# A complex linear recurrence and an MLP on one core: the two turned copies of a channel in neighbouring partitions, one load for the phases, and another order of all steps

## The chip, the core and the metric

The kernel runs on one core of one Trainium2 chip. The core has five instruction queues that run beside each other, each in its own order: TensorE (PE in the profile; its weight loads are PEld), VectorE (DVE), ScalarE (ACT), GpSimd (POOL) and SyncE (SP), which here issues every transfer. Sixteen DMA engines move the data. The metric is the device time of one launch in microseconds. Before the change it was 854.92 us in the median of three runs (851.49, 854.92 and 858.98).

## What is computed

First a gated linear recurrence for 4 batches, 8 heads, 768 tokens and 48 channels, with a complex gate per token and channel whose magnitude is held under 0.999; then a two-layer MLP on the result, with a leaky activation:

```
mag = np.sqrt(a_re * a_re + a_im * a_im)
scale = np.minimum(mag, 0.999) / (mag + 1e-06)
a_re_n, a_im_n = (a_re * scale, a_im * scale)
for t in range(S):                       # S_re, S_im: 48x48 for each batch and head
    new_re = ar * S_re - ai * S_im
    new_im = ar * S_im + ai * S_re
    S_re, S_im = (new_re + k[t] v[t]^T, new_im)
    y[t] = q[t] . S_re
x = y as (3072 tokens, 384)
h = x @ w_in                             # 384 -> 2048
out = (max(h, 0) + alpha * min(h, 0)) @ w_out
```

## The kernel before

**The recurrence.** Each batch is cut into 6 chunks of 128 tokens, so there are 24 units, (batch, chunk). In a unit the product of gates over a stretch of tokens is split in a magnitude (the decays) and a turn (the phases). A real 96-row problem replaces the complex 48-row one: q and k lie in a tile twice, 48 channels in partitions 0 to 47 and the same 48 again in partitions 48 to 95. The first copy is multiplied by the real part of the phase, the second by the imaginary part (L665, L667), and the matmuls sum over all 96 partitions. The six levels `LEVELS` (1, 2, 4, 8, 16, 32) multiply by decays on VectorE (L721), meet keys and queries on TensorE (L682, into `ps_lv`), mask (L703 on ScalarE, L706 on VectorE), and apply the values (L821, into `ps_y`). Keys are transposed (L789, copied by ScalarE at L791 and L792), and the state `St` goes on from chunk to chunk (L801, L830, L833, L845). The 48 rows of y are copied out (L859) and written to a DRAM scratch `ysc` (L864).

**The gates.** `gates` makes decays and phases for a whole batch or half of one, with 128 channels in partitions: 9 calls, A to I in the order, of 1, 2, 3 and then six times 3 chunks. It writes them to DRAM scratch tiles: `decs` (L324) and `phs` (L432, with the first token's value at L422). For batch 0 its small operations run on VectorE, for the others on GpSimd: products of 8 by 8 tokens (L339, L341), then a short serial recurrence over the tile `run`, six steps of an L339 and an L341 on 12 and 6 elements per partition for a call of 3 chunks. ScalarE hands it its input (`runs<-gate`, L367 and L369) and takes its output (`runs<-run`, the same lines a little later).

**The loads.** `loads` brings a unit's operands: q and k from the inputs into `KQ` (L580, L582; two copies each of 192 KB), phases from `phs` into `PP` (L591, two loads of 193.5 KB, real part into partitions 0 to 47, imaginary into 48 to 95), and decays from `decs` into `T` (L598, the same 384 KB twice). `KQ` has 3 buffers, `T` 2, `PP` 1. `loads_v` brings values in token order and spread by level (`V`, `VL`), `half_rows` makes a DRAM scratch `vsc` for some of these. `pieces` and `weights` load the float64 weights as words (L492) and turn them into float32 (L508, L510, L512 on ScalarE, L516 on GpSimd, L518, L520 on VectorE).

**The MLP.** `loads_x` loads a group of 128 or 256 tokens (L877). `all_mlp` runs over 14 groups: for each of 16 features blocks, three matmuls (L893, `ps_h`, two buffers), the activation by ScalarE (L900) and VectorE (L902) into `g_sb`, then the second layer's matmuls (L912, `ps_o`), and the result goes out (L922, L925).

**The order.** Each of these functions is a generator that yields before each step. `ORDER` is a string of 4316 letters; a letter names a generator (A to I gates, J loads, K half_rows, L loads_v, M pieces, N and O the weights, P to Z and a to m the 24 units, n loads_x, o the MLP) and lets it go one step on. So the string fixes the order of all instructions on all five queues. The arguments of the yields (costs, rings) are not used when the string is run.

Of the kernel before, what the change touches and what calls it, by code (L numbers as in the profile page):

```python
# [27 lines left out]


ORDER = (  # L30
    "AAAAAAAAAAAAAAAAAAAAABAAAAJMJJMABBBMMBANJMMAOAAAAAAAAAAAAAAAAAALLLNBLAAAAAAAAAAALNAAAAAAAKKKKKKKLLLA"
    "OALLAMNNAAAAAAOAAAAAAAAABLBNAAAAAAALAANBBNOOBNBBBLBMBBBJJOJNOBBBBBNBBJNNNBBNBBBBOBBBBBBBBBBBBBBBNOPB"
    "POBPPPPCCCBOKBBBBBBBBBBBBBPPOBBPKBCBBBMPCBPKKBCBJKKOPOPBBBBBBOMBKPNPMBBKNJBCKBBBBPPMBKKNKKBBNBPBBBBP"
    "PBCCBPPOPCCCPPPNNPPCCCCPPCPPPPJLPPPPPJNCJPCNNNCCJNCNCCQJQJPQJDDJJCPCJMNCNCPCPCPPCOCQQPDQDDJPPPPOCOOO"
    "CJKQCQCCCCCCQQCCCCCMOQCOJCJRCCRCOQOCOQQCQCOOOCCCCCCNNKKMMCCOCQCRCQCQCNNNKCLLLLLLQLCCCCCRQOCnCDCCCOCO"
    "CCCCQRMLLNDCJQCNRNRLLCQCCLLLRMCQCQDQRJJOCOCKQODCCCCRDNQQQQCCQQQQQQJODMQLNNDQODDODoQEKoooooooDOoRooND"
    "JoooooooDRRQQRQLLoooDNoooJLoRLLLLLDRLOQNQooQoQLooRRoRoDDoQDQDOOLDoooDDoRDELDLRRRRORRRRRJDooDDDDDDDRo"
    "ooRNNooDDRooooooEoRDRRRRRDNDoDoESDSDRDJOSREKOoooooLnoLLKoRSoooRRRRSSOLLKLSSSooESRLooooooLRoSOLLoLJEL"
    "LSooNJSSSSoEoEESSDooDDooDDDDDDooooDDDDDDDKJREEoooDDDDooEDDDSDDoEooEoooSSSRSSSoLSooooJJSJETSJSJJooKJS"
    "oEoooDDDDDDooDESDSoooSSSDDDSSJEEoEETSSSSDESSSoSSSTEoooooooJJJoKoEooDSDTooooEoSoTUKTLoTTTLoooooooooLT"  # L40
    "LoLoDKUooooooLDDTDJJooooJJnKDDDoEEooooDooTTETooDooooooLUoooooooooEoTToooUUDDLoooooooDTooToooooooDLDU"
    "UUooooooUTUUooooooUoTTTTEoUUTTTTEooTTUToLLLLoooEEEToLooTTTTTTJJTTUoUUoTTUJoEooTETTTTTJKEUUUUUFooooEU"
    "oooLLVooEoUooLLLELULLUVUoTUTVooUEEoooEULLLLLoooUUUJJJFEEUUUUUJJVVVUVVooooVVVJoUUUUUVVooFVooooUooVVoV"
    "FFVVoFVLLVooEEEEEEEEEEEEEEEEoooEEEEoooooFFJJoWVLLVWJFVoooJooooVooVVVVVWVoLVFooWoFoEEEoEVoVLWWLLLLLLE"
    "LLVWVnVooJJEEEEEEJJFWooFEEEEEoWWoFFVFVJVFWVJVoFoVooooooEWEWFVLVLVWWVWVVVVoooLKLooLLLoLLLJFFWWoXoWLJo"
    "EEoEEELEoooooEooJooWWoEWEWWWEoooWEoEoooWWooFoWoWFoooooEXWWoooooLXoFoooooFFXoLXXWWWWXXWXFEXWXWWWXJJoo"
    "oooJXXJJXFWXXFFFFoWWWWWoXoXooLoooWooooooXWLXXXXXooFoooXXFYoLLFFFFFFFoXXooXoXXoooLLLLLLLoooLLLYXXXJJX"
    "FJXFFFFFFFFFFFooXYGooXXXGooYoooXXnFYJXXYYoFooYYXXXXYGooooYJJJooooooooooJoJJYFFFFooJoooJooYYYYLGGoGZY"
    "YoooooooGGoFFFFFFFooooFoYZoooFooFFoZooooZYYZYYZGYYZZoYYYoGZoYFFoYoooKKLLoYLLLLZLoLLLJLFFFFFLFLFFoZGG"
    "YoooooGZooGGoGGYYoYYJJJYoKKYGooYFFoFKKYoYLYLYLFLLLLYYLLLLFGaGZoYZFYYYFZZLZGKooooZooooLLoZKooFFFFFooo"  # L50
    "ooZZZZaZZZZZooooZZoooooZooZoooJJFFGnooJoZZZZZFFFLooLFFZLZoZJLLLoGoaaGooooooooaZZaaGGJoGoooaooaLHaHao"
    "oGGoooGGGooaooooooooZZaZGGZZZoZaaaaaGGoooaHJoGoooooooaaaoaGGaaGaaaoooooGGaoLoaLoJJoooooHHGboGGGGGGGa"
    "oHoaooLLobooLLoooooJHHabJabHaaaaaabaJbJJaJaJaHaaabbbbbbbbHJKoooooooHoooooooJGGGGoGGbbbHbGGooocGGGGbJ"
    "HoooooooooooJGGGKoooHbbccoooooooooobbccbGGGHcGbobbbGcGoooGGGGGGGGGHccooobbHGbGKLooooHHboobLLJLLLLLoL"
    "LLLLbLKnoobbcccHbbHJbcbcGHHHbHHbbcJoHHLLLLLLooLoLJLLHHHcooooocccHHoooooooooHGGGGbbbbbbbboGccccccGGoc"
    "GJGooocLoooooGocLoccooooocLLGoGHGGooocJoooocGcccccccccccccJcccooKdooHooHoooJJJoHHHoJooHHHodHHHHooooo"
    "ooooooHHHHdHHHHHooHHdoodddJdJJddddJJooeooooooooooooddoodddoooeoooddHHoooooooooHddeeeeoHHHHHLHHHHHHHL"
    "LLdddLLLLLdLLLLoJLooeeddddodooHHddoJJeoooHdddHdddddneoooHHoIddeeeeeoodeJJfLfIHdHHdHeddddooooeHooooLL"
    "LLooooooJJoooIIoooeooooIoooHoHHHooeeIoeeeHHHLfILoooHIooLooeIofHeJJoeooeooooIfffefoooeeLofoLoLoeLLLee"
    "eeeeeeoJHfKHJJooooooofeoILLfooIeeHffffKLLLfoeJLooeeeeeooooooofoooooooofoooLoofKffgooooffffffIffLILLL"  # L60
    "LJooIgHooooLfLfoooIooIKKIIIIoffffIfJnJfJHgfgJofIJJoooooooJfoooooogIfggfgoLoooffIIfLfffIogoKoggoooooo"
    "ooooooohhoogoooogggggoIhJhggoooooLoJoooooooooohhLJJooooghggggggghohogIILIIoogIoooggIogLLLLooooooIohh"
    "hhhooooLLLLgIoKKgggggggggJJJhhooohogggLIoooooooooIIIIIIKKoooogoghoJIoooooioooLooooiJJIIoooooonIIIooh"
    "hhoiioooIIIIIoIhhhIIhhhLLLLLLLhhhiJiooILLLLLooIhJooohiohhooIIooooiiJhhhhhhIhIIiohooooiooLoLiLLLILiJI"
    "hhIhhhhhJiiIiiiiooIIIIIIIIIoooooooooooLiiiiIoIooooohhiiiiiioooJjiooIIIIoooooIIoLjJJjjLooooLIooLiLoLL"
    "IjjjooooIooijjjjIIoooooooiiiIiIIiiooiLooioooLLLiLLILoLLLIIjoiiijjoiiiioooIiojoooooooooojjjoooooooono"
    "jjjoooojjLjjjjjoooooIjLjLLooooooojjoojjjjjjoooJJJJJJoooJJoojJJjoooookokkJJoooooooooooojkjkLLjjjkjjoj"
    "jkkoJkkJoJJJkoookooooLLLooooooooJlJlkkooooooooookokklooklokooooooloolkkkkokkklllLooookookLkoloLJkooo"
    "ooooooLLkLLkLoLoooollkkkkkkkkkkkkkkkoooooooooollllllooJoooooookkolooooollollJmmnJJloooooooomooollooo"
    "oooooollmllooooommllooooooooooLLoLLoLoooLLLLLoLLLLooooomooooooommmmmoooollllllooolloooooolllllllllmm"  # L70
    "oooooooooLooLLLoooommooooooooooooooooLoooooomoooooomooooLLLLLLLLmooonooooooooooommommooooooooooooooo"
    "oooooooooommmmmmooooooooooooooooommmooooooooooooooommmmmmmmmmmmomoommnoooooooooooooooooooooooooooooo"
    "oooooooooooooooooooooooooooooooooooooooooooooooooooooooooooooooooooooooooooooooooooooooooooooooooooo"
    "oooooooooooooooo")
# [930 lines left out]
```

## Time and profile before

| | |
|---|---|
| median of three runs | 854.92 us |
| profiled execution, first to last instruction | 851.8 us |
| instructions of PE, DVE, ACT, POOL | 11488, 1020, 937, 293 |
| busy: PE, DVE, ACT, POOL | 697.3, 653.9, 439.5, 206.6 us |
| DMA queue of SP | 194440 packets, 129.20 MB, busy for 64.0% of 16 engines' span |
| mean granted TensorE clock | 0.956 |

A fp32 matmul stands in the profile as two records, so the 768 records of L912 are 384 matmuls. The costliest groups of the page: line, engine, operation, what is written from what, shapes, count, then busy us and mean ns of one, then the engine's idle time before them and what ended it.

```profile
L912 PE MATMUL ps_o<-w_out_sb,g_sb 128*128 128x384 f32 x768 | 295.8, 498 | 12.8 <-DVE g_sb L902 10.0
L893 PE MATMUL ps_h<-xT,w_in_sb 128*128 128x256 f32 (+1 forms) x1344 | 299.5, 355 | 0.0
L721 DVE TENSOR_TENSOR KQ<-KQ,T 96x1024 f32<-96x1024 f32 x120 | 147.3, 1231 | 31.5 <-PE ps_lv L682 25.1
```

The three kinds of loads that the change touches, with the phases' and decays' writes, in the page's list of transfers (count, KB of each):

```profile
T<-decs SPq DMA_DIRECT2D x48, 384.0 KB
PP<-phs SPq DMA_DIRECT2D x48, 193.5 KB
KQ<-in_q_dram SPq DMA_DIRECT2D x48, 192.0 KB
```

### The profile page before, as it was taken

The numbers are of one execution on the slowest core, as the hardware profiler recorded it, in microseconds if no ns is written. First come the engines' busy times: TensorE is split into PE (matmuls) and PEld (weight loads), VectorE is DVE, ScalarE is ACT, GpSimd is POOL, SyncE is SP. The second block draws the span as 40 slices with busy tenths as digits, with TensorE's granted clock in tenths as the row PEclk, the third lists the DMA queues.
The fourth block names the chain that finished last, engine by engine and source line by source line (L and its number), as shares of the span: only waits on it lengthen the run. The fifth ranks groups of instructions, "written<-read, shape, count | busy, mean of one in ns | idle before, by whom it ended". The sixth has DMA issues, their size and how long they took to land.

```text
span 851.8 us, 26881 instructions
## 1 busy us (share of the span) xinstructions
PE 697.3 (82%) x11488; PEld 530.0 (62%) x11488; DVE 653.9 (77%) x1020; ACT 439.5 (52%) x937; POOL 206.6 (24%) x293
## 2 busy tenths in 40 slices
PE   0001414776998899899999999999999999999998
PEld 0001313565776677677777777777777777777776
DVE  5999999997997899599989986987776756633212
ACT  6767758766346754575476436554444334322221
POOL 6131232466403810270046044000052000000000
PEclk9999656798999999999999999999999999999999
DMA  8697977856779576877875887687554486412010
GB/s 238 140 286 173 245 187 232 221 133 134 179 192 197 120 164 171 185 159 168 240 152 130 219 157 183 146 189 177 130 119 99 142 157 124 89 44 65 11 39 9
DMA packets 194559, 130.92 MB, mean 154 GB/s; under 512 B 74504, under 2 KB 186248, under 8 KB 194440
## 3 DMA queue, kind: packets, MB, share of 16 engines
q1 hardware_dynamic: 194440, 129.20, 64.0%
q8 instruction: 90, 1.47, 0.8%
q14 instruction: 29, 0.24, 0.1%
HBM read 100.82 MB, written 35.71 MB: 160 GB/s over the span
## 4 chain that ended last, share of the span: by engine, by line
PE 58%; DVE 25%; DMA 7%; issue 3%; ACT 3%; SPq 3%; POOL 1%; DVEq 0%; ACTq 0%; POOLq 0%
PE ps_o L912 23%; PE ps_h L893 22%; DVE KQ L721 5%; PE ps_lv L682 4%; DVE gate L339 4%; DMA T<-decs 3%; PE ps_y L821 3%; DVE gate L427 2%; DVE gate L341 2%; PE ps_y L845 2%; PE ps_kv L801 2%; SPq L630 1%; DVE g_sb L902 1%; PE ps_kt L789 1%; DVE gate L430 1%
## 5 line engine op out<-in xcount | busy, mean ns | idle before, releaser
L912 PE MATMUL ps_o<-w_out_sb,g_sb 128*128 128x384 f32 x768 | 295.8, 498 | 12.8 <-DVE g_sb L902 10.0
L893 PE MATMUL ps_h<-xT,w_in_sb 128*128 128x256 f32 (+1 forms) x1344 | 299.5, 355 | 0.0
L893 PEld LDWEIGHTS ps_h<-xT,w_in_sb 128*128 128x128 f32 x1344 | 233.7, 192 | 71.1 <-issue 1.8
L902 DVE SCALAR_TENSOR_TENSOR g_sb<-g_sb,al,ps_h 128x256 f32<-128x256 f32 (+1 forms) x224 | 97.3, 436 | 131.6 <-ACT g_sb L900 131.2
L900 ACT ACTIVATE g_sb<-ps_h 128x256 f32<-128x256 f32 (+1 forms) x224 | 79.0, 354 | 201.5 <-PE ps_h L893 200.7
L912 PEld LDWEIGHTS ps_o<-w_out_sb,g_sb 128*128 128x128 f32 x768 | 137.1, 191 | 63.6 <-DVE g_sb L902 12.9
L721 DVE TENSOR_TENSOR KQ<-KQ,T 96x1024 f32<-96x1024 f32 x120 | 147.3, 1231 | 31.5 <-PE ps_lv L682 25.1
L682 PE MATMUL ps_lv<-WQ 96*32 96x32 f32 x2304 | 34.7, 204 | 79.3 <-DVE WQ L665 51.9
L682 PEld LDWEIGHTS ps_lv<-WQ 96*32 96x32 f32 x2304 | 26.8, 116 | 97.0 <-DVE WQ L665 51.9
L339 POOL TENSOR_TENSOR gate<-gate 128x72 f32<-128x72 f32 x42 | 23.9, 569 | 147.6 <-ACT gate L369 144.7
L744 ACT COPY WQ<-KQ 96x1024 f32<-96x1024 f32 x48 | 50.0, 1042 | 14.9 <-DVE KQ L721 14.8
L516 POOL TENSOR_SCALAR top<-top 128x768 f32<-128x768 f32 x16 | 39.2, 2454 | 70.1 <-ACT top L508 70.1
L760 ACT COPY W<-KQ 96x512 f32<-96x512 f32 x48 | 30.8, 642 | 43.7 <-DVE KQ L721 37.3
L339 DVE TENSOR_TENSOR gate<-gate 128x576 f32<-128x576 f32 (+5 forms) x84 | 49.9, 594 | 1.7
L859 ACT COPY T<-ps_y 48x256 f32<-48x256 f32 x96 | 30.8, 366 | 38.9 <-PE ps_y L845 38.3
L821 PE MATMUL ps_y<-A,VL 64*48 64x64 f32 x2304 | 43.3, 229 | 7.0 <-issue 5.6
L821 PEld LDWEIGHTS ps_y<-A,VL 64*48 64x48 f32 x2304 | 41.3, 129 | 7.9 <-issue 6.4
L789 PE MATMUL ps_kt<-ident,KQ 96*128 96x96 f32 x192 | 26.4, 263 | 22.3 <-DVE KQ L721 12.2
L427 DVE TENSOR_TENSOR gate<-gate 128x1152 f32<-128x1152 f32 (+2 forms) x36 | 44.2, 1250 | 0.1
L703 ACT ACTIVATE A<-ps_lv,columns 128x64 f32<-128x64 f32 x144 | 37.3, 336 | 13.0 <-PE ps_lv L682 12.8
L789 PEld LDWEIGHTS ps_kt<-ident,KQ 96*128 96x128 f32 x192 | 22.3, 150 | 30.9 <-ACT T L792 10.9
L801 PEld LDWEIGHTS ps_kv<-V,T 64*64 64x64 f32 x1408 | 28.0, 148 | 15.4 <-ACT T L792 8.7
(106 smaller groups left out, 927.2 us busy)
## 6 DMA issues: line engine op xcount, KB each, us to landing
T<-decs SPq DMA_DIRECT2D x48, 384.0 KB
PP<-phs SPq DMA_DIRECT2D x48, 193.5 KB
KQ<-in_q_dram SPq DMA_DIRECT2D x48, 192.0 KB
decs<-gate SPq DMA_DIRECT2D x7, 1152.0 KB
phs<-gate SPq DMA_DIRECT2D x14, 576.0 KB
KQ<-in_k_dram SPq DMA_DIRECT2D x40, 192.0 KB
vsc<-in_v_dram SPq DMA_DIRECT2D x48, 144.0 KB
VL<-vsc SPq DMA_DIRECT2D x24, 288.0 KB
```

The costliest lines, as they stand in the source:

```text
L339: on(4 * k).tensor_tensor(out=m, in0=w[:, 1::-1].unsqueeze(2).to_broadcast([P, 2, 2, k]), in1=pairs_of(u), op=ALU.mult)
L427: TT(out=m[:, a], in0=U5[:, 1 + a], in1=turned(off3, o)[:, a].unsqueeze(1).unsqueeze(3).to_broadcast([P, L // 2, nb, 2]), op=ALU.mult)
L682: nc.tensor.matmul(t[64 * i + j:64 * i + j + HC // 2, p], lhsT=keys(n, g), rhs=queries(n, g), start=True, stop=True)
L721: nc.vector.tensor_tensor(out=x, in0=x if x0 is None else x0, in1=m, op=ALU.mult)
L744: nc.scalar.copy(z.rearrange("p i n t -> p i (n t)").rearrange("p i (m h) -> p m i h", h=h), bass.AP(tensor=KQ.tensor, offset=KQ.offset + ...
L789: nc.tensor.transpose(t[:, p], KQ[:, 1, 4 * i + p], ident[:D2, :D2])
L801: nc.tensor.matmul(kv[s][j:j + HC, n], lhsT=T[rows, n, j:j + HC], rhs=V[rows, n // 2, (n % 2) * D:(n % 2 + 1) * D], start=True, stop=True)
L821: nc.tensor.matmul(o, lhsT=Vp[h][64 * i:64 * i + 64, s, e_ * D:(e_ + 1) * D], rhs=a, start=False, stop=False)
L893: nc.tensor.matmul(p, lhsT=w_in_sb[:, f // 2, kk, f % 2 * P:(f % 2 + 1) * P], rhs=x_of[m][:, kk], start=(kk == 0), stop=(kk == NK - 1))
L900: nc.scalar.activation(gt, p, AF.Relu, scale=-1.0)
L902: nc.vector.scalar_tensor_tensor(out=gt, in0=gt, scalar=al_1[:, f:f + 1], in1=p, op0=ALU.mult, op1=ALU.add)
L912: nc.tensor.matmul(sums[0], lhsT=gt[:, c * P:(c + 1) * P], rhs=w_out_sb[:, f], start=(f == 0), stop=(f == NF - 1))
```

## The change

The row of channel d and copy i in a 96-partition tile is now 2d + i instead of 48i + d. A load of one copy of `KQ` or `T` therefore writes partitions 0, 2, ... 94 or 1, 3, ... 95 (`slice(i, D2, 2)`); it still has 48 rows and as many bytes. The scratch `phs` gets the part index inside the channel, so that one load of 96 rows and 387 KB fills `PP`, where two loads of 48 rows did. `start` (the first token's keys) is written with the same step. The operations on VectorE, ScalarE and TensorE keep their shapes, since all of them treat the 96 rows alike or sum over them. SP issues 731 transfers instead of 755.

`ORDER` is another string, of 4292 letters: 24 J fewer, the count of every other letter the same. Every queue's order differs. The lines below the string move up by one in the new file (gates), and by four after `loads`.

```diff
-        phs = dram.tile([2, H * D, n + 1], F32, tag="phs", name="phs")
+        phs = dram.tile([H * D, 2, n + 1], F32, tag="phs", name="phs")
...
-            nc.sync.dma_start(phs[o, :, 0:1].rearrange("(t p) s -> p t s", p=P), begin[:, o].unsqueeze(2))
+            nc.sync.dma_start(phs[:, o, 0:1].rearrange("(t p) s -> p t s", p=P), begin[:, o].unsqueeze(2))
...
-            nc.sync.dma_start(phs[o, :, 1:n + 1].rearrange("(t p) s -> p t s", p=P), p.rearrange("p (t s) -> p t s", t=NK))
+            nc.sync.dma_start(phs[:, o, 1:n + 1].rearrange("(t p) s -> p t s", p=P), p.rearrange("p (t s) -> p t s", t=NK))
...
-            nc.sync.dma_start(start[0:D], kv_in[:, :, :, 0].rearrange("b d h -> d b h"))
+            nc.sync.dma_start(start[0:D2:2], kv_in[:, :, :, 0].rearrange("b d h -> d b h"))
...
             for i in range(2):
-                rows = slice(i * D, (i + 1) * D)
+                rows = slice(i, D2, 2)
                 if i:
                     yield DMA(196)
                 nc.sync.dma_start(KQ[rows, 0], qv[b, :, :, cols])
...
-            for i in range(2):
-                rows = slice(i * D, (i + 1) * D)
-                t = yield DMA(196, ("PP", u), takes=() if i else (R["PP"],))
-                scr, phs, at = scr_of[u]
-                if i == 0:
-                    L["PP"] = PP = work.tile([D2, H, P + 1], F32, tag="PP", name="PP", bufs=1)
-                nc.sync.dma_start(PP[rows], phs[i].rearrange("(h d) s -> d h s", d=D)[:, :, at * P:(at + 1) * P + 1])
+            t = yield DMA(393, ("PP", u), takes=(R["PP"],))
+            scr, phs, at = scr_of[u]
+            L["PP"] = PP = work.tile([D2, H, P + 1], F32, tag="PP", name="PP", bufs=1)
+            nc.sync.dma_start(PP, phs.rearrange("(h d) i s -> (d i) h s", d=D)[:, :, at * P:(at + 1) * P + 1])
             done["rotation", u] = t
             for i in range(2):
-                rows = slice(i * D, (i + 1) * D)
+                rows = slice(i, D2, 2)
                 t = yield DMA(393, ("T", u), takes=() if i else (R["T"],))
```

The start of the two strings, for their look (the rest differs as much):

```diff
-    "AAAAAAAAAAAAAAAAAAAAABAAAAJMJJMABBBMMBANJMMAOAAAAAAAAAAAAAAAAAALLLNBLAAAAAAAAAAALNAAAAAAAKKKKKKKLLLA"
+    "AAAAAAAAAAAAAABBAJAMAAAMMMNMAMKAAKAKOAKAKAAAAAAABABABANAAAAAAAANNNAABKKKKKKKKKKAAAAAAAAJABANAJBBBAAB"
```

What of the built order the text speaks of, counted in VectorE time: each instruction is given the mean length of its row in the profile before, and the point of another queue's instruction is the sum over the VectorE instructions that stand before it in the program. `T`'s second half is issued this long before the first multiplication that reads it (L721), for the first twelve units:

| unit | 0 | 1 | 2 | 3 | 4 | 5 | 6 | 7 | 8 | 9 | 10 | 11 |
|---|---|---|---|---|---|---|---|---|---|---|---|---|
| before, us | 0.7 | 0.5 | 0.2 | 0.0 | 6.6 | 0.0 | 0.0 | 0.4 | 0.0 | 0.0 | 3.2 | 0.0 |
| after, us | 1.0 | 8.9 | 0.0 | 0.9 | 0.0 | 11.4 | 0.9 | 1.6 | 0.0 | 0.0 | 0.0 | 7.6 |

More of the change, by code (lines that the diff above doesn't have):

```diff
@@ L30 @@
 ORDER = (
-    "AAAAAAAAAAAAAAAAAAAAABAAAAJMJJMABBBMMBANJMMAOAAAAAAAAAAAAAAAAAALLLNBLAAAAAAAAAAALNAAAAAAAKKKKKKKLLLA"
[L32 to L74, printed above, removed]
+    "AAAAAAAAAAAAAABBAJAMAAAMMMNMAMKAAKAKOAKAKAAAAAAABABABANAAAAAAAANNNAABKKKKKKKKKKAAAAAAAAJABANAJBBBAAB"
+    "BBBAAAABBAOBMABABNBBAAAAABJBBAABABBABAABBKBABAOBAAAAANNOBBMABABANBAABABABBBAOBOBBBBBBBBBBLBNBBBNNBMN"
@@ new lines @@
+    "BBJBCCNNNBOBBBPBBOOOJPBBOBJNBCBPBJBBBOBCPCLLLLBKPBBMLLOJLMPLLCCBBBBJLLLCPPPOBOBLCBBPBBNBBCBBMCCCOPPP"
+    "NNDPCCCCCCCPCOPPPPPDCCCKDOCJOJPCJJJQCJKMJOQPPCPPPPPPPPPPDDOCCCNNNNPNPPCJJOOKCDDDKOCPPPPKOMOCNQNCMDPC"
+    "ONCPCNCQLPPOPPPPPQLLLNNMNNCQQCQLQQCDCCCDDDPPCQCMOnCOCNCLNCLLRLLLCLQOOOOOCJOOOCNQQQCQCQCKQQQKCQDNDKOO"
+    "CCCRCDDNNJJLoCQoCooooDCLDDoCQQQQQQQQQQQMQQQQQCRCQDMDDCOKCNCQCKNCNKLQQKQLCLLLLLCLCCDQQQQCDCDDCJoooooo"
+    "QoooRoDoCDDLLLLDCCDCRRRRCCRCCDCCCDCCCCRRRCDQJRRoJRoooNDoRooORRLCooOOROooooODRRRRDRooRRRRoooooDooDLRR"
@@ new lines @@
+    "JSDooRooSNNoDoooooEREoJoJRRRREDRRooEEDRSoDoDooooLoLRooooRoRNNDDDooEDSSSoSooJJoLLJJoJoooRSSSSoooLRRRn"
+    "RROOooooSooSSSSoooRoLLooTESSSooLLoJoLooTDDDDDDDDDDSDDSSoEEESSSSoSLLLoJooLoSSSTooooooESoSooToTSESSSDJ"
+    "DDDSSJEJEJJEESESLLLLoooSLSoTTSTTSSSSSSooJnooUoooTooJTJJooDDDDDDDDDDDDDDDoDooJoEoLLLoDoTooooooooETTDo"
+    "oToEoooooUooooLLooLLooDTTTLLJooToooooDDDDDoDTTDoTTToDToooooTTTTToooDDDooTToooooDEooDTDoooEEoKEoooooo"
+    "UEooooooFFJEEEEEETTTTTETEEoTEoooooooEoTTTTTTTTLTEoEoUoELoLoLLUoooLLLFoooEEELoFEoEEEUoooUoULLLLooooUU"
@@ new lines @@
+    "UoooooFFoUoooUFUUooUoUoEEEUooUooooooUUUUUUUUUooJJJJooVVVVoooVUoUKKKKEKEEEEEEEEEEEEEEEEEEEEoUUFJooUUU"
+    "UUUVoKLULFVVoVVUUUUUUUUoJFJVEoEVEEEVooooFoVoooEEEEEEooLVVLoVooVoooWVVnooooJJLLVoLEoooLLooEVEWooEELVV"
+    "VVVVLLLoVoVLoooJoEEoWooEEEVJJJooEVVooWWWWWWVVVVVVWVWLLooLJVVLLKooooFWEoWWEoLLVVVVVLoVWoLLLVWVWoWooXo"
+    "VoooWoXooooLWoWWLLooooEEJWWWWWWFWooooWooWoJoWJJEWWWFWFWFFEFLLLLLLJLWXooooXFooooooooFWFJFFFLFLLLoooJW"
+    "oWLoFXXFXFFWWWWXWWWWLFoFooXXXoFoooFooooooXXXXXXoXoXoFoooLooFooooXXoFXXJooJFoYYYoGonXXXXXXooooooooooF"
@@ new lines @@
+    "XXoooXooGYGJGFFFFJJGXXXJXXXFXFKKKYYFFFFFFFFFFXFXXXXXXYYJXXXooooGYooooYooooYYooooooZJJFoYYFoYYoLYoooo"
+    "LGLZLLLGZGLLLLLLLLYYoooooooZZZYZYYYYZYZZYYoZoooYooYJYooZFoFFFFFFFFFFFFFFFoFJoYooYYYYGYYGGYYYGYZZZZZJ"
+    "YJYYYYYYFYGoGFJoFFFFoJJoJJooooooZZooooJoaaJooooLFoFooGLLLLGFZLLZLZZLZZLLLoFooooLoGoooooFLoGoFFooFZoo"
+    "aFFFZoZooooGFFoooooGooooGooaZooZKoKoKFFFGZFooFooGoZnFZZZZZZLaaLZZZZZZZLZoGaZZZGoooaaaGaGooooLLLoooao"
+    "ooLJGoGooGGGaGGaoaoooooooGGoooKooooaaaaooooaaGGooGaoHHoGoGaaaaHGGGGGGGGGGGGGGbGbGLLLbLooaaaaooooooLL"
@@ new lines @@
+    "oooooooaoaooJJoHHoaaaabbbHaaabbabbKaHKJHJJJKoJooobKaKHHaaaaaJooGJGGGGGGGGGGGGJJoocoooocooooHooobHooG"
+    "GobLLLooGooooobbGbbbboobGocooGGGGGooooooooLbLLLooooLLooHnLLbcbbcLLLcooJbbbbbbbbocoJoobJoobbcccbbbbbc"
+    "cbbbccccLcccLLLLLLbGbbbbbbLLLoooooooooodooooLLobccHcHccdccoooocoooooooLLHooHooHcHccooooocooocJcccGcG"
+    "cocccJGoooGLGJoGcodGGdGGGHdddcdcdcccccLoooodoooooooHooodoooooLooLLLLLLoGGLGGLKLLoGooJJdJocoHdodJddHJ"
+    "JooooooJoLHHHHHoJodoooodooooodnHHHHHHHHoooooooooIIdddodHdoooddddodoedooddoooddddddLLeLeeKLeLLHeLLddd"
@@ new lines @@
+    "ddoeedeeeLdLddoooLooLHoooooddKeJeHeJooJeoJoJHoJoJeoeeoooHoHHHHoHeHoHHoHoooHoHeeeeoooooooooooofoooooo"
+    "oooeeeeeeeooffoofeooeHHHLHHHHHHHHHIHHoHHHoHHffHLHfefHoffffeHeHeHeeHeoHooooIHfffHfefeeeJfeeoooLHLLLLH"
+    "JJLLLLLoLeeeeooooJLfooLJIIooooofJffofooLoooooggooHHHHHHHHfffoHoooooIooIoooooHfJfoofofHnoogHHHooooooo"
+    "foofgfffffggfooHffffIfIIIIJoooooJfooffffJfooJooooJogoogILogoLoooogoggoohoohooooooghgKKKKggggKKKooooo"
+    "ooooooLhLhhLoLoLooooIooooogIoIoooooLLooLLoghhgoggggIgIKogoIooooogggLLoohhJhgghhoooooggohgggghLghggIJ"
@@ new lines @@
+    "oIJIJIIIIIIIIoghhhoogggggoooooohIJohoonoIoJooohhIoohIoIoIIooohhhhhIhooIoIoooooILLLhhLoLLLoLLLoLLLIoo"
+    "oooioooJoooIoIoIIIhoooooiohoohihhohhhhhhioiiiihhhohJhhhhoLoiioooooooJoLLioiiiIooIoooIoiIiIIiLoIiILII"
+    "IIIIIIIIIIIIIIIIIioooJoJJiiiiiiiJiJooJooLooLLLLLLLLooiooooooooiooooIooIIjIjijiiojoiiiiiLijijijijojij"
+    "jLoLiLoLoIIIooIooIIIoLoooLLoooLjjIjjjoooIIjjjILoLoIooLooLoooooLooiiiiiiooooooIIIoooInojjjoIIIJJJoooJ"
+    "ooooooojjjjjJjjjooooooooooooooooojooJjjjjjjjjjjjjjJJkjjjjjkJkoookLoooJoJJooJkkokkkokkLoooooLoolooool"
@@ new lines @@
+    "okkkkkoolooJoLoookLLLLLoooLoLLLkkolooJooooklLkloooooooookkkkokoooooooolooookkookkooooookoJokkkkJkkll"
+    "lllkllkkkkkkkokkokkoooLLLooooooloolooonooooooooooooooooooooooooooooloooooJoJJoooooooooooooooommmmooo"
+    "oooooloooloooooooooooooolmlmllLLLLoooooooooollmlomoooollLLLLLLLolloooooooololollllllmmmmlmmLlllllmlm"
+    "llloooooooooooooooooooommomlnoooooooooooooLLLLmLmLmmmmLLoomLLLLommooooooooomoomooooooooooooooooooooo"
+    "ooooooooooooooooooooooooooomoomoommmmmmmmmmmmmooooooooomomooooooooooonoooooooooooooooooooooooooooooo"
@@ L77 @@
+    "oooooooooooooooooooooooooooooooooooooooooooooooooooooooooooooooooooooooooooooooooooooooooooo")
 class Ring:
```

## The prediction, made before the changed kernel was run

> **What bounds the kernel now.** I read the slices first, then busy time by stretch, then who waited, then single stretches of the engines.
>
> ```profile
> PE   0001414776998899899999999999999999999998
> DVE  5999999997997899599989986987776756633212
> DMA  8697977856779576877875887687554486412010
> ...
> DVE KQ L721 <- DMA T<-decs: 6.0, 3, 2.5
> DVE gate L260 <- ACT gate L258: 5.4, 1, 5.4
> ```
>
> The slices (21.3 us each, busy tenths) show a hand-over: VectorE is full for some 300 us while TensorE has little to do, then TensorE is full to the end. A stall of VectorE before the hand-over or of TensorE after it lengthens the run, one for one; most others cost nothing. Around the hand-over both are nearly full, so it is no point but a stretch.
>
> To compare the two built orders I gave every VectorE instruction before a point, and every TensorE matmul from a point on, the mean time that its row occupies its engine (without overlaps: 653.9 and 699.8 us in all), and took the points where a matmul waits for VectorE. The largest sum before is 835.3: 276.0 of VectorE up to an L902, and 559.3 of TensorE from the L893 that waits for it, among it 330 of L912 at 0.676 (223.0) and 516 of L893 (213.5). The means count early matmuls, run at a lower clock (0.73 granted from 64 to 128 us), too cheap, and late ones too dear; with each one's own time the largest sum is 817.5. Of the span of 851.8, 34.3 is then idle time: 9 at the start (VectorE waits 0.9, 5.4 and 2.4 us for the first gates), 3.8 in the last 72 us, and 21.5 between. The change can win from those 21.5, or from the sum.
>
> **The sum.** The same count on the new order gives 834.0: 221.8 of VectorE (31 L721 for 36.1, 34 L902 for 10.5, gates and weights the rest) and 612.2 of TensorE (351 L912 for 237.2, 567 L893 for 236.5). That is 1.3 us less. Shapes and counts are unchanged, so nothing else can move it. Near 300 us of VectorE the new sum is 829.6 against 834.3: VectorE's stalls late in the hand-over have 4 us of cover which they lack now.
>
> **The step of two.** These are the rows of five stretches (length; busy time of each engine; clock; DMA share; GB/s).
>
> ```profile
> core 0: us, PE busy (x) PEld busy (x) DVE busy (x) ACT busy (x) POOL busy (x), PEclk, DMA share, GB/s
> 10.00:13.00 3.00, 0.00 (x0) 0.00 (x0) 2.86 (x11) 1.66 (x3) 1.65 (x5) 1.00 1.03 343
> 15.00:19.00 4.00, 0.00 (x0) 0.00 (x0) 3.65 (x11) 3.81 (x5) 0.86 (x1) 1.00 1.04 381
> 81.50:87.00 5.50, 2.23 (x52) 1.93 (x54) 5.50 (x7) 3.08 (x8) 0.12 (x1) 1.00 1.14 182
> 221.50:224.00 2.50, 2.50 (x74) 1.97 (x73) 2.50 (x4) 0.91 (x3) 2.44 (x1) 1.00 1.14 193
> 256.00:263.00 7.00, 6.98 (x212) 5.88 (x210) 5.11 (x9) 2.02 (x6) 1.89 (x6) 1.00 1.07 201
> ```
>
> In the first two, 128-partition transfers (gates, weights, the decays' write) move 343 and 381 GB/s. In the other three it is PP and T, 48 partitions each, and the engines are as busy for 182 to 201. Packet size is not the cause: packets of 1024 B take 46 ns around 18.5 us and 88 to 139 ns while T is loaded. So a load of 48 neighbouring rows is held up where it lands, and at its worst (near 134 GB/s at 83.5 and 135 at 222 us) while the first half is under way. A T pair of 786 kB takes 4.1 us at 193 GB/s and would take 2.3 at 343. Half of the rows in every second partition is neither; I take 3.0, a gain of 1.1 for a pair, with bounds of 0 and 1.8.
>
> [...]
>
> What is that worth? Only the waits that it ends. VectorE waited for T three times, 1.27 at 227, 2.51 at 264 and 2.25 at 343 us, 6.0 in all; the rest of T's time had other VectorE work above it. Each shortened by 1.1 leaves 2.7. The order matters too: of the first twelve units, ten issued T's second half at most 1.0 us of VectorE time ahead of use (the table), in the new order eight; 8/10 of 2.7 is 2.2, or, with the 4 us of cover for the last of the three, 1.9. So 4.1 us less; bounds 0 and 6.0. VL's loads, for which TensorE waited 1.33 us once, are not in the step; 0 taken, bound 1.3.
>
> **One load for the phases.** 24 issues of about 0.41 us leave SP's queue; SP waits for others, so 0. If its cover were gone, one issue is 0.4 us for a unit. L665 needed both halves before and needs the whole now; 0. KQ's loads (18.9 MB) become faster as well, but stand up to 40 us ahead of use: 0. `start` is read once: 0.
>
> **The order.** The largest single gap of TensorE after 191 us is no transfer but GpSimd's recurrence of gates D:
>
> ```profile
> 193.04 0.23 POOL L339 TENSOR_TENSOR gate<-run,runs 128x12 f32<-128x12 f32 x1
> 193.34 2.52 POOL L341 TENSOR_TENSOR run<-gate 128x6 f32<-128x6 f32 x1
> 195.94 0.23 POOL L339 TENSOR_TENSOR gate<-run,runs 128x12 f32<-128x12 f32 x1
> 196.25 2.45 POOL L341 TENSOR_TENSOR run<-gate 128x6 f32<-128x6 f32 x1
> ...
> 198.78 2.75 POOL L339 TENSOR_TENSOR gate<-run,runs 128x12 f32<-128x12 f32 x1
> ...
> 205.16 2.05 PE L801 MATMUL ps_kv<-V,T 64*64 64x48 f32 x63 [4.70 <-ACT T L792]
> ```
>
> The same tiny operation takes 0.23 us or over 2, as VectorE's long two-input operations run beside it. Six steps took 12.6 us; ScalarE stood 4.91 us at `runs<-run`, with the T copies (L791, L792) and an L900 queued behind, TensorE 4.70 behind those, and VectorE 2.78 at L833. The old order gave this recurrence 8.7 us of TensorE time between the L900s around it, the new one 15.2, and 16 instead of 6 of VectorE. The gap should go; it lies before the new hand-over, where VectorE's idle counts: 2.8 less (bounds 0 and 4.7). What is late next is gates E: its recurrence took 14 us, and the room between L900s shrinks from 17.5 to 11.4. That can cost up to 2.6; taken 1.3. F, G, H and I took 7 to 10 us and have 10.9 to 18.7. The other waits, some 10 us, will be different ones; I take them as equal, having no row for the new.
>
> **Sum.** 851.8 - 1.3 - 4.1 - 2.8 + 1.3 = 844.9 for the span; 3.1 lie between it and the median, so **848.0**, 0.8% less.
>
> **Rivals.**
> - *The order is worth more.* With faster loads the other waits go too. 21.5 less the 8.8 named above leaves 12.7; half of it gone is another 6.4: 841.6. For it: VL from vsc was issued at no distance from its use in the first six units, now 0 to 20 us ahead, and ScalarE has room. Against: waits of 0.5 to 2.6 us with many causes.
> - *The step does nothing*, since something else slows these loads (they read 512 and 1024 B runs of DRAM). Then 4.1 is lost: 852.1. Against: the 46 ns packets.
> - *T behind the gates: slower.* In the new order units 0 and 3 issue T directly behind two gate loads of 574 KB; before, T stood directly behind PP in unit 0. 1.18 MB at 343 and T at 193 GB/s are 7.5 us, against 5.5 and 4.4 us of VectorE work between first issue and use: 2.0 and 3.1 late, before the hand-over, so they count. At 182 GB/s for all, 10.8 each: 5.3 + 6.4 = 11.7, and T's gain is off: 852.1 + 11.7 = 863.8. It breaks even once these two waits exceed 6.9 us together. For it: at 81.5 us T shared the engines with such loads, at 182. Against: gate loads land in 128 partitions, and KQ's and PP's are out of the way by then.
>
> **How the numbers follow.** The forecast has 0.54, with a range of its own from 842 to 853 (terms at their bounds); the better order 0.16, the idle step 0.10, T behind the gates, or another wait of the new order as large, 0.20. A difference of 1%, 8.5 us, is about what a measurement can tell. Faster by more is 0.45 of the forecast and all of the better order, 0.40; slower by more is the last case, 0.20; within, 0.40. The range, 838 to 864, takes in the better order with D's full 4.7, and the slower rival.
>
> **What would show it.** Stretches with T and PP at 250 GB/s or more; DMA share under 60%; VectorE's waits for T near 2 us in all; no gap of TensorE at L801 behind `runs<-run` of D, perhaps one at E; TensorE full from about 225 us on. I am wrong if T stays near 190 GB/s, or if VectorE idles over 15 us before 200, or TensorE over 15 after 250.

## The result, and the profile after

The changed kernel takes 875.25 us (median of 4 runs, 872.59 to 880.48) against 855.44 before (851.49 to 858.98): a ratio of 1.0248, 95% interval 1.0213 to 1.0282. It is slower by 20 us, outside the range of the prediction. The profiled execution has a span of 878.5 us, 26.7 more than before; it is the longest of the four (the others have 870.7 to 874.7), so a trace shows some 7 us more than the medians do. Line numbers after L590 are 4 lower now, those of the gates 1 lower: L721 is L717, L821 is L817, L893 is L889, L912 is L908.

The slices and the transfer queues of the changed kernel:

```profile
PE   0001324989998899899989989989999989899998
DVE  5999999998989779799867966858856746344212
DMA  6799875775667667377664575545735374132110
...
q1 hardware_dynamic: 194056, 129.20, 55.7%
q8 instruction: 90, 1.47, 0.7%
```

The same 129.20 MB now keep the DMA engines busy for 55.7% of the span instead of 64.0%, so the loads did become faster. TensorE is busy some 50 us earlier (from about 160 us on instead of 210), but then it does not stay full: the unbroken nines of before have become a row of nines and eights. What TensorE waited for (us in total, times, longest), first before, then after the change:

```profile
PE ps_y L821 <- issue: 5.6, 3, 3.2
PE ps_o L912 <- issue: 2.5, 1, 2.5
```

```profile
PE ps_lv L678 <- ACT WQ L740: 33.0, 5, 9.8
PE ps_lv L678 <- ACT W L756: 24.5, 5, 8.4
PE ps_y L817 <- issue: 16.4, 10, 3.0
PE ps_y L841 <- issue: 11.9, 7, 4.4
PE ps_lv L678 <- issue: 5.4, 3, 2.9
```

"Issue" means that nothing in the profile released the instruction: no engine, no transfer of data. These waits went from 8.4 to 33.7 us in the whole span, and from 4.9 to 32.9 after 250 us. The waits for ScalarE in the first two lines of the second list lie before 200 us and cost little; they are needed below. One such stall, in the changed kernel's timeline of TensorE (start, us, operation, records; in brackets the idle time before it):

```profile
707.15 1.15 PE L797 MATMUL ps_kv<-V,T 64*64 64x48 f32 x64
708.12 0.29 PE L808 MATMUL ps_y<-ident,nothing 64*48 64x256 bf16 x4
708.23 1.52 PE L817 MATMUL ps_y<-A,VL 64*48 64x64 f32 x96
709.68 0.59 PE L841 MATMUL ps_y<-KQ,St 96*48 96x64 f32 x13
714.64 1.30 PE L841 MATMUL ps_y<-KQ,St 96*48 96x64 f32 x19 [4.37 <-issue]
```

TensorE stops in the middle of L841, after 13 of 32 equal records. What follows is slow too. The stretches around it (length; busy time of PE, PEld, DVE, ACT, POOL; clock; DMA share; GB/s):

```profile
709.50:713.00 3.50, 0.77 (x33) 0.54 (x21) 2.91 (x3) 0.00 (x0) 0.00 (x0) 1.00 1.10 264
713.00:716.40 3.40, 1.76 (x20) 1.59 (x21) 1.22 (x1) 0.37 (x2) 0.11 (x1) 0.55 0.08 20
716.40:719.80 3.40, 3.40 (x8) 2.36 (x7) 0.48 (x1) 1.95 (x5) 0.00 (x0) 0.50 0.40 94
719.80:723.20 3.40, 3.40 (x75) 2.44 (x74) 0.76 (x1) 0.13 (x1) 0.00 (x0) 0.94 1.03 252
```

The granted clock stands at 0.50 for 6.83 us from 713.4 on, so up to 3.4 us more are lost. And while TensorE stands, the engines first are full of data (share 1.10): the one packet of queue q8, TensorE's instructions (90 packets in the run, for 23,223 of them), starts at 712.05, 1.8 us after TensorE ran out, and TensorE goes on 2.6 us after that.

### The profile page after: what moved, and what is told of

Its sections match the earlier page's. It is cut to its first block, busy times and chain, and to the rows that moved or that the text cites. A ratio compares the mean times of both kernels' runs of the same rounds, so it can differ in the third digit from the quotient of the medians.

```text
span 878.5 us, 26844 instructions
## 1 busy us (share of the span) xinstructions
PE 708.6 (81%) x11488; PEld 537.8 (61%) x11488; DVE 652.2 (74%) x1020; ACT 441.3 (50%) x937; POOL 186.0 (21%) x293
## 3 DMA queue, kind: packets, MB, share of 16 engines
q1 hardware_dynamic: 194056, 129.20, 55.7%
## 4 chain that ended last, share of the span: by engine, by line
PE 69%; DVE 12%; DMA 6%; issue 6%; ACT 3%; SPq 3%; POOL 1%; DVEq 0%; ACTq 0%; POOLq 0%
PE ps_o L908 27%; PE ps_h L889 26%; PE ps_lv L678 4%; PE ps_y L817 4%; PE ps_y L841 3%; PE ps_kv L797 3%; DVE KQ L717 2%; PE ps_kt L785 2%; DVE gate L426 1%; DVE gate L338 1%; SPq L626 1%; DMA St<-in_v_dram 1%; DVE gate L340 1%; DMA ysc<-T 1%; DMA T<-decs 1%
## 5 line engine op out<-in xcount | busy, mean ns | idle before, releaser
L889 PE MATMUL ps_h<-xT,w_in_sb 128*128 128x256 f32 (+1 forms) x1344 | 304.6, 359 | 0.5 <-DMA xT<-ysc 0.5
L908 PE MATMUL ps_o<-w_out_sb,g_sb 128*128 128x384 f32 x768 | 301.1, 508 | 3.4 <-DVE g_sb L898 3.0
L889 PEld LDWEIGHTS ps_h<-xT,w_in_sb 128*128 128x128 f32 x1344 | 236.9, 195 | 74.1 <-issue 3.2
L717 DVE TENSOR_TENSOR KQ<-KQ,T 96x1024 f32<-96x1024 f32 x120 | 148.0, 1235 | 45.2 <-PE ps_lv L678 30.9
L908 PEld LDWEIGHTS ps_o<-w_out_sb,g_sb 128*128 128x128 f32 x768 | 141.9, 196 | 59.2 <-DVE g_sb L898 6.2
L817 PE MATMUL ps_y<-A,VL 64*48 64x64 f32 x2304 | 45.3, 230 | 17.9 <-issue 16.4
L515 POOL TENSOR_SCALAR top<-top 128x768 f32<-128x768 f32 x16 | 43.4, 2714 | 50.8 <-ACT top L507 50.2
L817 PEld LDWEIGHTS ps_y<-A,VL 64*48 64x48 f32 x2304 | 42.1, 130 | 19.6 <-issue 17.9
L338 DVE TENSOR_TENSOR gate<-gate 128x576 f32<-128x576 f32 (+5 forms) x84 | 48.1, 572 | 2.5 <-ACT gate L310 1.2
L678 PE MATMUL ps_lv<-KQ,W 96*32 96x32 f32 x1536 | 24.7, 204 | 25.7 <-ACT W L756 24.5
L841 PE MATMUL ps_y<-KQ,St 96*48 96x64 f32 x768 | 31.6, 233 | 12.0 <-issue 11.9
L702 DVE TENSOR_TENSOR A<-ps_lv,mask 128x256 f32<-128x256 f32 x96 | 37.2, 412 | 0.0
```

Of the source, the lines that this page charges most:

```text
L338: on(4 * k).tensor_tensor(out=m, in0=w[:, 1::-1].unsqueeze(2).to_broadcast([P, 2, 2, k]), in1=pairs_of(u), op=ALU.mult)
L515: nc.gpsimd.tensor_scalar(out=top, in0=top, scalar1=F64_SMALL, scalar2=None, op0=ALU.max)
L678: nc.tensor.matmul(t[64 * i + j:64 * i + j + HC // 2, p], lhsT=keys(n, g), rhs=queries(n, g), start=True, stop=True)
L717: nc.vector.tensor_tensor(out=x, in0=x if x0 is None else x0, in1=m, op=ALU.mult)
L817: nc.tensor.matmul(o, lhsT=Vp[h][64 * i:64 * i + 64, s, e_ * D:(e_ + 1) * D], rhs=a, start=False, stop=False)
L841: nc.tensor.matmul(Y[64 * (n % 2):64 * (n % 2) + D, n // 4, n // 2 % 2, HC * s:HC * (s + 1)], lhsT=before[:, n], rhs=KQ[:, 0, n, HC * s:HC ...
```

## Where the 27 us come from

From 250 us on TensorE sets the end. I valued the matmul passes that each execution still had to do at that time by one price list, the mean start-to-start times in the run with the old order and the new loads (shown next), and split the rest of the time:

```
profiled execution        span   from 250  work left  no releaser  other waits  low clock
before                    851.8    601.8     582.9        4.9          5.5          3.3
old order, new loads      852.9    602.9     581.2        5.1          6.1          6.4
changed kernel            878.5    628.5     570.1       32.9          2.1         19.6
```

The last column is what passes took longer while the clock was at one half; some 4 to 5 us of each row are in none of the columns. At 250 us the changed kernel is 582.9 - 570.1 = 12.8 us ahead of the kernel before. It then gives back 24.6 in waits (35.0 against 10.4) and 16.3 in the clock: 28.1 more, against 26.7 in the spans. How the passes are priced matters by about a microsecond: by kind of pass alone the lead is 11.7. The traces of the second and third row are the longest executions of their kernels.

## The experiments

My theory after the traces was that TensorE runs out of instructions in long rows of small matmuls. A fp32 matmul is four instructions (two passes, each a weight load and a matmul: the 384 matmuls of L908 are 768 records of PE and 768 of PEld), and a unit's matmuls are short: in the rows of the small ones TensorE starts a pass every 15 ns on average, against 250 ns in the MLP. The new order puts 520 such instructions in a row ten times after the hand-over; the old one has no row above 456 (528 and 464 in the expectations, which take four instructions for every small matmul). The rivals were the new layout of the loads, and values that come late.

**Order and loads by themselves.** The old order with the new loads, and the new order with the old loads; the string of letters gets one J (a step of the loads) less or more for a unit.

```diff
# old order, new loads: a unit's steps of the loads, in the order of before
-JJJJ JJ JJ      q k q k, PP PP, T T
+JJJJ J JJ       q k q k, PP, T T
```

> The changed loads with the order of before (its letters unchanged, less one phase load a unit). Theory (instruction supply): the loss is in the new order's long rows of small matmuls, which leave TensorE without instructions; this order has none of 520 instructions, so 846 to 856 us, TensorE's gaps with no releaser after 300 us at most 6 us in all. Rival 1 (the loads in steps of two do harm): 868 to 880. Rival 2 (in the new order the values come late behind other loads): 846 to 856 as well; the next two runs tell it from the theory.

Measured: 848.3 us, ratio to before 0.9909 (0.9878 to 0.9940), 5.1 us of waits without a releaser after 300.

> The loads of before with the new order (one more letter a unit for the second phase load). Theory (instruction supply): the same rows of small matmuls, so about the same gaps without a releaser after 300 us (20 to 30 us in all), and T slower again: 872 to 888 us. Rival 1 (the loads in steps of two do harm): 848 to 858, gaps under 8 us. Rival 2 (values late): 872 to 888.

Measured: 901.2 us, 1.0477 (1.0421 to 1.0533), 36.8 us of such waits after 300 (in the longest of its four executions, 908.4 us, the one traced). So the loads help, by 0.9% in the old order and by 2.2% in the new one, and the order alone does the harm. The first rival is out. The second has little room: in the changed kernel TensorE waited for values (`VL`) once, 1.5 us. The time of the second run, above what was expected, is taken up below.

**Rows broken.** In these runs ORDER's next letters o (the MLP) move forward into the rows.

> The changed kernel; wherever more than 200 instructions of small matmuls stood in a row, the next steps of the MLP, up to two of its matmuls, are pulled forward between them (148 steps moved; the order is otherwise the same, and so is every load). Theory (instruction supply): the gaps without a releaser after 300 us fall from 28 us to under 8, and the kernel takes 842 to 856 us. Rivals 1 and 2 (loads, values late): the loads are as before, 868 to 880.

> The kernel of before with the same edit of its order (108 steps moved). Theory (instruction supply): little to win, its gaps without a releaser are some 5 us in all from 200 us on: 846 to 856 us. If pulling MLP steps forward does harm of its own (they wait for VectorE or ScalarE), 858 or more; then the run before this one has to be read with that cost taken off.

Measured: 877.1 us (1.0233) and 869.9 us (1.0153). The waits without a releaser after 300 did fall, to 7.7 and 0.3 us, but other waits came: after 250 us they are 12.1 us in the new order, 7.4 of them for ScalarE's `W`, and 14.8 in the old one, 5.4 of them for VL. (The new order's 10.3 us for x lie at 105 us, long before TensorE sets the end.) Both kernels also begin the MLP earlier in the loading of its weights, with 17 of 24 writes of `w_in_sb` done at the first matmul instead of 19 and 20, so I repeated the edit later in the order and away from those loads.

> The changed kernel with rows of small matmuls broken at 280 instructions, from the 850th step of the order on only, two matmuls of the MLP to a break, and none of them the first of a group whose x was loaded less than 250 steps before (91 steps pulled forward, 30 breaks). The first broken order pulled steps ahead of the loads they need: it read weights that were not there yet, and its TensorE waited 10.3 us for x. Theory (instruction supply): gaps without a releaser after 300 us under 8 us instead of 28, no new wait for x; 30 breaks may cost 0.1 to 0.2 us each, as the busy time of the first broken orders suggests (9 us more TensorE time for some 40 and 55 breaks): 850 to 860 us. Rival (values late, or the loads): 868 to 880.

> The same with rows broken at 400 instructions only (49 steps, 15 breaks: the rows of 520 and 456, each once). Theory (instruction supply): a row of 400 is still longer than what was fetched ahead in most places; gaps without a releaser after 300 us between 8 and 22 us, 856 to 872. If the breaks themselves were what helped, half of the breaks would give half of the gain of the run before this one; if only rows over 456 stall, all of the gain comes with these 15.

Measured: 874.9 us (1.0233, 1.0183 to 1.0283) and 869.0 us (1.0167, 1.0117 to 1.0217); waits without a releaser after 300 of 13.8 and 20.4 us. Twice as many breaks gave less, against the expectation: 30 breaks cost TensorE 6.7 us by longer passes and brought 10.6 us of other waits. The length of rows was not the whole story.

**Boundaries.** Tiny matmuls ahead of everything else, when TensorE has nothing to do, move every later instruction by half a packet or by a whole one.

```diff
+early = ps.tile([P, 2, HP, HC // 2], F32, tag="lv", name="ps_lv", bufs=2)
+for i in range(64):                       # 128 for a whole packet
+    nc.tensor.matmul(early[0:D].rearrange("p i n t -> p (i n t)"), lhsT=nothing[0:64],
+                     rhs=ident.bitcast(BF16)[0:64], start=True, stop=True)
 plan.run(ORDER)
```

> The changed kernel with 64 tiny matmuls (128 instructions, half of a 16 KB instruction packet) before all others on TensorE, in time when it is idle; order and loads unchanged. Theory (instruction supply): the packets begin at other places of each row, so the gaps without a releaser come at other instructions than in the changed kernel, and their sum after 300 us changes by over 4 us, up or down: 856 to 890 us. Rivals (loads, values late): the same gaps at the same instructions, 871 to 881.

> The same with 128 tiny matmuls (256 instructions, a whole packet). Theory (instruction supply): every packet begins where it did, relative to each row; the gaps come at the same instructions as in the changed kernel, the sum after 300 us is 28 us within 4, and the time 870 to 882 us. Rivals: the same.

Measured: 867.3 us (1.0177, 1.0096 to 1.0258) and 880.5 us (1.0301, 1.0240 to 1.0362); waits without a releaser after 300 of 22.7 and 28.7 us. The place from the first timeline, with a whole packet ahead, and with half a packet:

```profile
705.46 0.59 PE L841 MATMUL ps_y<-KQ,St 96*48 96x64 f32 x13
710.42 1.30 PE L841 MATMUL ps_y<-KQ,St 96*48 96x64 f32 x19 [4.37 <-issue]
```

```profile
700.69 1.10 PE L841 MATMUL ps_y<-KQ,St 96*48 96x64 f32 x32
```

With 256 instructions ahead TensorE stops after the same 13 records, with 128 not at all. I then numbered TensorE's instructions (weight loads, passes and its own waits) and took for each wait over 0.6 us without a releaser, after 200 us, the number of the instruction that it held up:

```
                          waits   numbers, first ones                    modulo 256
before                       2    6339  8131                             195, 195
changed kernel              18    5571  6339  7106  8130  9155  9411 ...  all 194 or 195
new order, 128 ahead        16    5571  6339  8387  9411 10179 11202 ...  all 194 or 195
new order, 256 ahead        18    5827  6595  7362  8386  9411  9667 ...  all 194 or 195
new order, old loads        19    3522  5314  6339  7106  8130  9155 ...  all 194 or 195
```

With 256 ahead the first numbers are exactly 256 higher than without. Counted in the same way, the 19 traces of this study hold 163 such waits, all at 194 or 195. So all of these stalls lie at one place of every 256 instructions, and 90 packets of 16,384 B for 23,223 instructions are one for 258: I take that place as the boundary of a packet. The old order was then tried in the same way.

> The kernel with the old order and the new loads (848 us) and 64 tiny matmuls (128 instructions) before all others on TensorE. Theory (instruction supply): the gaps without a releaser move to other rows; their sum after 300 us, 5 us before, stays within 2 to 14, since this order has no row above 464 instructions: 843 to 860 us, less spread by the shift than the new order (867 and 875 to 880). If 840 to 846, it beats both kernels. Rivals: 848 within 3.

> The kernel with the old order and the new loads and 128 tiny matmuls (256 instructions, one packet) before all others on TensorE. With 64 of them (half a packet) it took 880 us. Theory (blocks): the boundaries stand where they stood in the 848 us kernel, so 845 to 854, gaps without a releaser after 300 us under 8 us. Rival (the tiny matmuls themselves do harm, by the clock or at the start): 876 or more.

Measured: 880.5 us (1.0262, 1.0170 to 1.0354), with 21.8 us of such waits after 300, and 852.2 us (0.9954, 0.9924 to 0.9984), with 1.5 us. The longest rows of their waits, 128 ahead and then 256 ahead:

```profile
PE ps_y L817 <- issue: 14.5, 9, 2.6
PE ps_lv L678 <- issue: 11.4, 8, 4.0
```

```profile
PE ps_y L817 <- issue: 1.8, 1, 1.8
```

The first time was not expected: I had thought that an order without rows of 520 is safe. Half a packet of idle-time work makes the good order as slow as the changed kernel, a whole packet does not. What matters most is how long the 256 instructions between two boundaries take, and those without MLP matmuls are the short ones. Blocks without a single MLP pass, after 200 us: 14 in the changed kernel (13 of them ended in a stall), none in the old order with the new loads, 13 with 128 ahead of it (all 13 stalled). The changed kernel's other five stalls over 0.6 us came behind blocks with two to eight MLP passes, which took 2.6 to 4.6 us. Some of the blocks without one in the changed kernel:

```
block starts   its 256 took   stall behind it   both   DMA share in its first 3 us
   547.1 us       2.08 us         1.42           3.51        0.03
   364.6          2.31            1.42           3.73        0.00
   396.3          1.94            1.25           3.19        0.52
   336.6          2.08            0.82           2.90        0.94
   577.1          2.14            2.91           5.05        0.89
   278.1          2.29            2.98           5.27        0.83
   707.9          2.37            4.37           6.74        1.11
   457.0          3.41            0              3.41        0.01
```

Of the 14, block and stall together take 3.0 to 3.8 us where the DMA engines are half idle or more, and mostly 4.8 to 6.7 where they are busy. The last row, the only one without a stall, ran at a mean granted clock of 0.55, so that the block itself took about as long as others do with their stall.

The packets of q8 show the same from the other side. In all 18 stalls of the changed kernel over 0.6 us, after 200 us, TensorE goes on 2.2 to 2.9 us after the start of the packet that fell into the block or its stall. In the 13 stalled blocks without an MLP pass that packet starts 0.6 to 1.5 us into the block where the DMA engines are half idle, and 2.3 to 4.2 us into it in four of the five where they are busy. So a block that is over in 2 us is over before such a packet has come.

**Rows made, and data taken away.**

```diff
# old order, new loads: one of eight places (l a unit, o the MLP, L values)
-oooollllllooolloooooolllllllllmmoooooooooLooLLLooo
+oooolllllllllllllllllmmooooooooooooooooooLooLLLooo
```

> The kernel with the old order and the new loads (848 us), in which eight pairs of neighbouring rows of small matmuls, 192 to 336 instructions each, are joined by putting the MLP steps between them (3 to 8 matmuls) behind the second row: seven rows of 528 instructions and one of 592, as the changed kernel has them, 71 steps moved, nothing else. Theory (instruction supply): most of the eight rows stall, 1.2 to 3 us each, and the longer stalls cost as much again in the granted clock: 858 to 872 us, gaps without a releaser after 300 us from 5 to between 12 and 25. Rival (the loss of the new order lies elsewhere, values late or another wait): 845 to 852.

> The changed kernel; from unit 6 on the loads of T bring the last 16 bytes of each row only, into the tile that the unit but one before had (its decays are then not the unit's own). About 14 of 129 MB are not moved; the order and TensorE's instructions are the same. Question: do instruction packets wait behind data? In the changed kernel the stalls of 2 us and more had a DMA share of 0.77 to 1.17 in the two microseconds before their packet, those near 1.2 us often none. If so: as many stalls, but most of them 1.0 to 1.6 us; gaps without a releaser after 300 us 15 to 22 us instead of 28, low-clock time under 25 us instead of 44, 856 to 868 us. If the length of the row alone decides: the same gaps and 871 to 880 us. Rival (T or values late): 848 to 860 with the gaps of TensorE gone altogether.

Measured: 874.7 us (1.0217, 1.0108 to 1.0327) for the joined rows; after 250 us 11.2 us of waits without a releaser, 11.6 of others (4.7 of them for VectorE, which the old order with the new loads had 1.1 of) and 13.2 in the clock. So joined rows do harm, but only about half of the added waits are for instructions (6.1 us of some 12). With T cut: 866.1 us (1.0100, 1.0020 to 1.0181), 22.5 us of waits after 300, and low clock for 10.2 us after 250 instead of 42.3. There are still 18 stalls over 0.6 us, but the longest has fallen from 4.4 to 3.3 us, and at L841 (L845 there) from 4.4 to 1.7:

```profile
PE ps_y L845 <- issue: 10.9, 8, 1.7
```

So data traffic lengthens the stalls. That fits the higher cost of the old loads in the new order: in the traces its stalls add up to 43.3 us after 250 with the old loads, 32.9 with the new ones. Both traces are of the longest executions, and no run separates this from the loads' other effects.

**Can the new order be freed of it?** Three ways to put MLP steps into its short blocks: pulled forward, held back, and as whole features.

```diff
# whole features: one of 15 places
-oooololollllllmmmmlmmLlllllmlmllloooooooooooooooooooommoml
+oooololollllooooooollmmmmlmmLlllllmlmllloooooooooooooommml
```

> What the runs so far showed: each stall without a releaser begins at a TensorE instruction whose number is 194 or 195 modulo 256, a packet boundary, and the stalls come where the 256 instructions before it took under some 3.5 us. So not the row counts but the block of 256. Here MLP steps are pulled forward into the 28 blocks of the changed kernel that would take under 4.2 us, and nowhere else (171 steps, 1 to 6 matmuls each). Theory (blocks): gaps without a releaser after 300 us under 6 us, low-clock time under 15 us, 836 to 854 us for some 6 us of new breaks and a few us of waits on ScalarE. Rival (rows too long, or breaks as such): like the run with rows broken at 280, where as many breaks stood at other places, 868 to 878.

> The changed kernel with its short blocks filled the other way: MLP steps that stood ahead of a short block are held back into it (202 steps, 34 places; three short blocks stay, where a load of x is in the way), so no MLP step comes earlier than it did and ScalarE's evictions do not get ahead of the units' copies. When they were pulled forward, the gaps without a releaser fell from 28 to 4.4 us as expected, but 19.4 us of waits for ScalarE's copies came in their place and the time stayed at 878. Theory (blocks): gaps without a releaser after 300 us under 8 us, waits for ScalarE under 8 us, 840 to 860 us. If the new order has no room for the steps in any place, 865 to 880 with waits for VectorE or ScalarE instead of the gaps.

> The changed kernel; in 15 of its short blocks seven MLP steps are put in the middle (one feature: three matmuls of L889, ScalarE's and VectorE's step, two of L908; some 2.6 us of TensorE), taken out of the middle of a nearby stretch of 12 or more MLP matmuls. Since it is exactly one feature, every other place keeps the same kinds of steps, so the MLP matmuls that cover a copy of ScalarE stay. Short blocks (under 3.7 us) go from 21 to 7. Theory (blocks, and the waits of the two runs before came from moved cover): gaps without a releaser after 300 us under 10 us, waits for ScalarE under 6 us, 845 to 862 us. If the time stays at 870 to 886 with few such gaps, the new order is slow for a reason that the stalls only hide.

Measured: 878.7 us (1.0259), 885.5 us (1.0326) and 875.0 us (1.0228, 1.0166 to 1.0291). The waits without a releaser after 300 fell from 28.1 to 4.4, 6.0 and 9.4 us, and the time did not. In the first, the MLP's activations were put ahead of ScalarE's copies:

```profile
PE ps_lv L678 <- ACT WQ L740: 40.5, 11, 9.8
PE ps_lv L678 <- ACT W L756: 33.0, 15, 7.6
```

That is 16 us more than in the changed kernel, in 16 more waits, and the low clock came here as well (12.4 us). In the second the transposed keys (L797 behind T) came too early, 15.2 us in 15 waits (4.3 in 2 in the changed kernel). In the third, 7.6 us for VectorE and 5.2 for data appeared, 12.7 without a releaser stayed, and 8.8 us of the lead at 250 us were gone (578.9 of work left). All waits of TensorE after 250 us together are some 32, 35 and 28 us in the three, against 35 in the changed kernel: the stalls went, the sum mostly stayed. The expectation of the third had named just this, a time of 870 to 886 with few such waits, as the sign that the order is slow for a reason that the stalls only hide. The same fillings in the old order:

> The same edit on the kernel with the old order and the new loads (848 us): 11 blocks are under 4.2 us, only three of them under 3.1, and 40 steps are moved. Theory (blocks): its 5 us of gaps and some of the clock after them go, 841 to 849 us. If it is 853 or more, moved MLP steps cost more than such short blocks do.

> The kernel with the old order and the new loads (848 us) with its seven blocks under 3.9 us filled by steps held back (32 steps). Theory (blocks): at most the 5 us of its gaps and what the clock loses after them is to be had, 842 to 850 us; if held steps make the units' results late, 853 or more.

Measured: 854.3 us (0.9982, 0.9952 to 1.0012) and 852.4 us (0.9950, 0.9932 to 0.9969). Neither beats the order that it began from, so here the moved MLP steps cost at least what the short blocks did. The fastest kernel of the study is the old order with the new loads, 848.3 us.

## Why the prediction was wrong

- **The step that failed** is "The other waits, some 10 us, will be different ones; I take them as equal, having no row for the new." After 250 us they were 10.4 us before and 35.0 after, and the clock behind them, which the sum did not have, took 19.6 instead of 3.3. Nearly all of these waits, 32.9 us, are one mechanism: TensorE stands at a packet boundary, by all signs because its next instructions are not there yet (in the 18 stalls over 0.6 us it goes on 2.2 to 2.9 us after the start of a packet). In the profile before it is three waits for "issue" after 250 us (4.9 us; another of 3.2 lies at 90 us), which I counted into those 10 without asking what they were. The rows of 520 instructions could be read from the new order beforehand, but not what they cost: with 128 instructions ahead, rows of at most 456 cost as much.
- **The step of two (-4.1)** was right in kind, and larger. T's stretches in the changed kernel move over 250 GB/s with the DMA engines full, as two of them show:

```profile
205.50:209.00 3.50, 3.50 (x81) 2.83 (x80) 3.50 (x5) 0.28 (x1) 3.34 (x3) 1.00 1.06 286
247.50:250.00 2.50, 2.50 (x72) 1.87 (x71) 1.82 (x3) 1.82 (x7) 0.57 (x3) 1.00 1.09 258
```

  VectorE's waits for T fell from 6.0 to 1.9 us:

```profile
DVE KQ L717 <- DMA T<-decs: 1.9, 2, 1.4
```

  That is the 4.1 of the forecast. By itself the change of the loads, the step of two and the single phase load together, is worth 0.9% of 857.5 us, 7.8 (5.1 to 10.5); no run has one without the other, and where the gain beyond the waits for T lies is open, since the trace with the old order (852.9 us) is of the longest of its five executions. That the old order with the new loads takes 848.3 us, almost the 848.0 forecast for both changes, is chance.
- **The order (-1.3, -2.8, +1.3).** D's recurrence no longer holds TensorE, no gap behind that of gates E appeared (the two waits of L797 for `T` lie before 140 us), and the lead of 12.8 us at 250 us is nearly twice the 6.9 that all terms together gave. Up to the hand-over the sum had the right direction; the count of idle time behind it did not.
- **"TensorE full from about 225 us on"** is what was false; "over 15 us idle after 250" was named as the sign.
- **The slower rival** (T behind the gates) had the right side and the wrong cause: VectorE did not wait for T before 200 us at all (its two waits are at 425 and 713 us).
- **Open:** whether this order can be fast at all. With most of its instruction stalls gone it had other waits in all three trials, and each trial moved steps that covered something else; so it is shown where the changed kernel loses its time, and not that it would be fast without the stalls. One block without MLP passes in the kernel before (at 605.5 us, 2.3 us long) passed without a stall because its packet was early: it starts at 602.98 us, 2.5 us ahead of the block. Why so early is open too.

## What to carry to other kernels

Where TensorE is the bound and its matmuls are short, count its instructions: a stretch of 256 between two packet boundaries that lasts under some 3.5 us mostly ended in a stall here (118 of 143 after 200 us in the 19 traces), and so did four longer ones in the changed kernel (3.6 to 4.6 us, with a DMA share of 0.78 to 1.09 in them); 128 instructions put in ahead of all others moved all the boundaries. A wait for "issue" in the chain is therefore a number to follow up, not a remainder; and two changes that were measured together should be run apart once, since one of them can hide the other's gain.

## What the runs showed of the hardware

- TensorE's instructions come in packets of 16 KB (90 for 23,223 instructions, 0.9 to 1.7 us each), and they mostly start late when data fills the DMA engines (4.15 us into the block at 707.9 us with a share of 1.11, 1.1 us into the one at 547.1 with 0.03). The stalls keep to a spacing of 256 instructions (163 of 163 at 194 or 195 modulo 256), and 26 of the 27 blocks without MLP passes in two traces (the changed kernel, the old order with 128 ahead), each 1.9 to 3.8 us, ended in one.
- In the changed kernel the clock fell to one half after stalls of 1.57 us (ended at 651.4) and 2.19 us (ended at 457.0), for 3.41 and 6.83 us. Eleven of the trace's twelve low stretches lasted 3.41 us or a multiple of it; the twelfth runs into the end of the span. The clock did not fall after a wait of 1.49 us that ended at 620.3. What decides between them no run tested.
